# RWKV-7 attention with a squared-ReLU feed-forward layer: second layer's weights rounded later, feed-forward part begun one slot earlier, squares one step later

## The chip, the cores and the metric

The kernel runs on one core of one Trainium2 chip. The metric is the device time of one execution in microseconds (us). TensorE (PE) multiplies matrices, VectorE (DVE) and ScalarE (ACT) work elementwise, GpSimd (POOL) does a triangular solve here, and SyncE (SP) issues most of the transfers (DMA). Every engine works through its own instructions in the order in which the program lists them, and waits at the first one whose inputs are not there.

## The reference

```python
# attention: B, H, S, D = 4, 8, 768, 40
for t in range(S):
    y[:, :, t] = einsum('bhd,bhde->bhe', r_t, state)
    Sa = einsum('bhde,bhe->bhd', state, a_t)
    state = state * w_t - einsum('bhd,bhe->bhde', Sa, b_t) + einsum('bhd,bhe->bhde', v_t, k_t)
x = y.transpose(0, 2, 1, 3).reshape(3072, 320)
# feed-forward: w_in is 320 x 2048, w_out is 2048 x 320
h = maximum(x @ w_in, 0)
out = (h * h) @ w_out
```

`w_in` and `w_out` come as 64-bit floats, the other inputs as 32-bit floats. The kernel turns the 64-bit words into 32-bit floats itself, from their integer halves.

## The kernel before

The sequence is cut into 6 chunks of 128 steps for each of 4 batches: 24 pairs (chunk, batch), each handled in one *slot*. A barrier in the program's order separates slots; it costs no time by itself. What a slot holds is listed in the main loop:

```python
    TOTAL = 12
    ahead = {0: (4, 5), 1: (6, 7), 2: (8,), 3: (9,), 4: (10, 11), 5: (12, 13)}
    ahead.update({i: (i + 8,) for i in range(6, len(order) - 8)})
    share = {**{i: (0, 0) for i in range(B)}, B: (8, 4)}
    pieces_in = {0: (4, TOTAL), 1: (6, TOTAL), 2: (6, TOTAL), 3: (7, TOTAL), B: (4, 4)}
    for i in range(len(order)):
        n, begin = share.get(i, (10, 0))
        jobs = [(chain(i, g), 11, 0, TOTAL)]                     # the recurrence of this slot
        jobs.append((some(second, n), n, begin, TOTAL))          # n steps of the feed-forward part
        # prepare(m) for m in ahead[i]                           # decays and products of later slots
        # rest(i + 1)                                            # inputs of the next slot
        # rounding: 2 half-steps for each piece in pieces_in[i]  # weights from 64 to 32 bits
        weave(*jobs)                                             # spreads each job over 12 steps
        # when all of a unit's prepared slots are done: solve(unit) on GpSimd
```

The weights are rounded in 26 pieces: 10 wide ones of 512 columns for the first layer, then 16 of 320 columns, one for each 128 rows of `w_out`. A piece takes two ACT operations and five DVE operations. `hid` is the later home of the hidden layer, which lends room to the raw words until then; the numbers of finished pieces in `then` start the next fetch:

```python
    in_turn = [free_words[:, at:at + 2 * DM] for at in [4 * WI + 2 * DM * i for i in range(4)] + [2 * DM * i for i in range(3)]]
    ...
    def rounding():
        ...
            if before:
                nc.scalar.activation(bits, bits, Act.Relu, bias=lowest, scale=float(1 << 23))
            if n < len(pieces):
                nc.scalar.activation(dst, words[:, :, 0].bitcast(U32), Act.Copy, scale=2.0 ** -32)
            yield
            if before:
                nc.vector.scalar_tensor_tensor(d_.bitcast(I32), hi, -(1 << 31), bits, Alu.bitwise_and, Alu.bitwise_or)
                nc.vector.scalar_tensor_tensor(d_, mant, 2.0 ** -20, d_, Alu.mult, Alu.mult)
                # fetches of `then`
            if n < len(pieces):
                bits, mant = (psum(ps_f)[:, :dst.shape[-1]] for _ in range(2))
                nc.vector.tensor_scalar(bits, hi, 20, 0x7FF, Alu.logical_shift_right, Alu.bitwise_and)
                nc.vector.tensor_scalar(mant.bitcast(I32), hi, 0xFFFFF, 0x100000, Alu.bitwise_and, Alu.bitwise_or)
                nc.vector.tensor_tensor(mant, mant.bitcast(I32), dst, Alu.add)
            yield
```

The pool `ps_f` has two PSUM buffers, and the feed-forward part uses the same two. That part works on groups of three slots (384 tokens): 16 hidden steps, then three times 4 output steps of 4 matmuls each, 28 steps in all.

```python
    def ffn():
        for gi in range(len(order) // GB):
            while gi not in gathered or finished[0] < NARROW:
                yield False                                      # a step given away
            for f in range(0, NF, 2):
                ...                                              # two matmuls with w_third, for f and f + 1
                for e, p_ in enumerate(ps):
                    ...                                          # two matmuls with w_in
                    h_ = hidden[:, f + e]
                    nc.scalar.activation(h_, p_, Act.Relu)
                    nc.vector.tensor_tensor(h_, h_, h_, Alu.mult)
                    yield True
            while left():
                yield False                                      # until every piece is rounded
            for n in range(GB):
                ...                                              # 16 matmuls with w_out, a yield after every 4
                nc.scalar.copy(o_, p_); store(out[at:at + C, :], o_)
                yield True
```

At the end of every third slot the three slots' tokens are moved into the feed-forward part's layout by eight small transfers (`tokens<-tokens`); `gathered` is set two steps after these are listed. GpSimd's solve of a unit of 1, 2 or 4 slots reads its input back from HBM (`half_n<-kept_d`), works in `half_p` and `half_t`, and stores the result (`kept_t<-half_t`); the slots fetch it as `T<-kept_t`, over the queue of SyncE.

```python
    sizes = [1, 1] + [2] * 4 + [4] * ((len(order) - 12) // 4) + [2]   # units 0 to 9
    ...
            nc.gpsimd.tensor_tensor(p_, part[...], t3[...], Alu.mult)        # half_p
            nc.gpsimd.tensor_tensor(t3[...], t3[...], p_, Alu.subtract)      # half_t
```

Of the kernel before, what the change touches and what calls it, by code (L numbers as in the profile page):

```python
# [9 lines left out]
I32 = mybir.dt.int32  # L10
U32 = mybir.dt.uint32
Alu = mybir.AluOpType
# [5 lines left out]
def kernel(  # L18
# [22 lines left out]
    nc = tc.nc  # L41
    ctx.enter_context(tc.manual_schedule())
    B, H, S, D = r.shape
    DM = H * D
# [3 lines left out]
    HC = C // 2  # L48
# [3 lines left out]
    NF = DFF // 128  # L52
# [7 lines left out]
    at = 0  # L60
    for h, d, n in ((6, 0, D), (7, 0, D), (5, HALF, D - HALF)):
        while n:
            j, row, room_ = free[at]
            m_ = min(n, room_)
# [3 lines left out]
            d, n = d + m_, n - m_  # L68
# [11 lines left out]
    ps_f = ctx.enter_context(tc.tile_pool(name="ps_f", bufs=2, space=PSUM))  # L80

    def psum(pool):
        name = "ps_" + pool.name[-1]
        return pool.tile([128, 512], FP32, tag=name, name=name)

    def mm(o, l_, r_, start):
        nc.tensor.matmul(o, l_, r_, start=start, stop=True, skip_group_check=True)  # L87

    def single(name, shape):
        return const.tile(shape, FP32, tag=name, name=name)  # L90

    def new(name, shape, bufs):
        return work.tile(shape, FP32, tag=name, name=name, bufs=bufs)
# [4 lines left out]
    def later(fn, steps=2):  # L98
        line.append([steps, fn])
# [7 lines left out]
    def store(out_, in_, steps=2, queue=nc.sync):  # L107
        later(lambda: queue.dma_start(out=out_, in_=in_), steps)  # L108
# [77 lines left out]
    w_out = single("w_out", [128, NF, DM])  # L186

    WI = 512
# [9 lines left out]
    free_words = hidden.rearrange("p f t -> p (f t)")  # L198
# [1 line left out]
    nc.vector.memset(lowest, -896.0 * (1 << 23))  # L200
    wide = [room[:, 4 * WI * i:4 * WI * (i + 1)] for i in range(2)] + [free_words[:, :4 * WI]]

    in_turn = [free_words[:, at:at + 2 * DM] for at in [4 * WI + 2 * DM * i for i in range(4)] + [2 * DM * i for i in range(3)]]
    LENT = len(in_turn)


    runs = []
# [19 lines left out]
    NARROW = len(pieces)  # L227
    WIDE = len(fetches)
    for f in range(NF):
        fetchable(in_turn[f % LENT], [(0, 128, moe_w_out[f * 128:(f + 1) * 128, :])], [w_out[:, f, :]])  # L230

    then = {1: (3,), 2: (WIDE,), 3: (4,), 4: (WIDE + 1,), 5: (WIDE + 2,), 6: (WIDE + 3,), 7: (WIDE + 4,), 8: (WIDE + 5,),
            9: (WIDE + 6,)}
    then.update({NARROW + f: (WIDE + f + LENT,) for f in range(NF - LENT)})
    finished = [0]
    left = lambda: len(pieces) - finished[0]

    def fetch_weights(n, queue):
        raw, sources = fetches[n]
        for row, m_, src in sources:  # L240
            to = raw.bitcast(I32)[row:row + m_]
            if len(src.shape) == 3:
                to = to.rearrange("p (i c) -> p i c", i=src.shape[1])
            queue.dma_start(out=to, in_=src.bitcast(I32))

    def rounding():

        now = None
        for n in range(len(pieces) + 1):
            before, now = now, None  # L250
            if before:
                bits = before[-1]
                nc.scalar.activation(bits, bits, Act.Relu, bias=lowest, scale=float(1 << 23))
            if n < len(pieces):
                dst, raw = pieces[n]
                words = raw.rearrange("p (f e) -> p f e", e=2)
                nc.scalar.activation(dst, words[:, :, 0].bitcast(U32), Act.Copy, scale=2.0 ** -32)
            yield
            if before:
                d_, hi, mant, bits = before  # L260
                nc.vector.scalar_tensor_tensor(d_.bitcast(I32), hi, -(1 << 31), bits, Alu.bitwise_and, Alu.bitwise_or)  # L261
                nc.vector.scalar_tensor_tensor(d_, mant, 2.0 ** -20, d_, Alu.mult, Alu.mult)
                finished[0] += 1
                for m_ in then.get(n - 1, ()):
                    later(lambda m_=m_: fetch_weights(m_, nc.sync), 1)
            if n < len(pieces):
                hi = words[:, :, 1].bitcast(I32)
                bits, mant = (psum(ps_f)[:, :dst.shape[-1]] for _ in range(2))
                bits = bits.bitcast(I32)
                nc.vector.tensor_scalar(bits, hi, 20, 0x7FF, Alu.logical_shift_right, Alu.bitwise_and)  # L270
                nc.vector.tensor_scalar(mant.bitcast(I32), hi, 0xFFFFF, 0x100000, Alu.bitwise_and, Alu.bitwise_or)
                nc.vector.tensor_tensor(mant, mant.bitcast(I32), dst, Alu.add)
                now = dst, hi, mant, bits
            yield

    def as_they_are():
# [13 lines left out]
    Q = HC // 2  # L290
# [102 lines left out]


    given = single("half_n", [128, Q * (HC + Q)])
    solved = single("half_t", [128, Q * HC])

    part_of = lambda u: given[:, u % 3 * Q * Q:(u % 3 + 1) * Q * Q] if u < FINE else given

# [245 lines left out]

    PART = NF // 4

    def ffn():
        for gi in range(len(order) // GB):
            while gi not in gathered or finished[0] < NARROW:  # L650
                yield False
            t_ = tokens.pop(gi)
            hid = []
            for f in range(0, NF, 2):
                ps = [psum(ps_f if gi < len(order) // GB - 1 else ps_w)[:, :GB * C] for _ in range(2)]
                for e, p_ in enumerate(ps):
                    half = slice(e * DP, (e + 1) * DP)
                    mm(p_, w_third[half, f * 64:f * 64 + 128], t_[half, NT, :], True)
                for e, p_ in enumerate(ps):
                    for j in range(NT):  # L660
                        mm(p_, w_in[:, j, (f + e) * 128:(f + e + 1) * 128], t_[:, j, :], False)
                    h_ = hidden[:, f + e]
                    nc.scalar.activation(h_, p_, Act.Relu)  # L663
                    nc.vector.tensor_tensor(h_, h_, h_, Alu.mult)  # L664
                    hid.append(h_)
                    yield True
            while left():
                yield False
            for n in range(GB):
                bb, c = order[gi * GB + n]  # L670
                p_ = psum(ps_f if gi < len(order) // GB - 1 else ps_w)[:, :DM]
                for f in range(NF):
                    mm(p_, hid[f][:, n * C:(n + 1) * C], w_out[:, f], f == 0)
                    if f % PART == PART - 1 and f < NF - 1:
                        yield True
                o_ = new("o", [128, DM], 2)
                nc.scalar.copy(o_, p_)
                at = bb * S + c * C
                store(out[at:at + C, :], o_)
                yield True  # L680

    second = ffn()
    gathered = set()

# [92 lines left out]
    TOTAL = 12  # L779
    ahead = {0: (4, 5), 1: (6, 7), 2: (8,), 3: (9,), 4: (10, 11), 5: (12, 13)}  # L780
    ahead.update({i: (i + 8,) for i in range(6, len(order) - 8)})
    share = {**{i: (0, 0) for i in range(B)}, B: (8, 4)}
    pieces_in = {0: (4, TOTAL), 1: (6, TOTAL), 2: (6, TOTAL), 3: (7, TOTAL), B: (4, 4)}
    done = set(range(B))
    unit = unit_of[B]
    for i in range(len(order)):
        bb, c = order[i]
        n, begin = share.get(i, (10, 0))
# [13 lines left out]
        if i in pieces_in:  # L802
            m_, end = pieces_in[i]
# [39 lines left out]
```

## Time and profile before

| | before |
|---|---|
| median of 3 runs | 1058.01 us (1055.46 to 1059.7) |
| span of the profiled run | 1058.2 us |
| PE busy | 943.7 us, 89% |
| POOL busy | 668.4 us, 63% |
| DVE busy | 500.5 us, 47% |
| ACT busy | 272.4 us, 26% |
| mean granted TensorE clock | 0.901 |

A slot ends where DVE scales its output (`tokens<-ps_c,dec`, L636). In this profile slot 0 ends at 89.7 us, slots 1 to 5 end at 139.0, 184.7, 222.8, 268.5 and 319.0 us, and slot 23 ends at 989.7 us. After that the last group of the feed-forward part stands alone. PE is the engine with the most busy time, but matmuls are pipelined and their ends are modelled, so that a busy PE is not always PE at its peak. GpSimd's spans are rough.

### The profile page before, as it was taken

How to read it: one execution, taken by the hardware profiler on the slowest of the kernel's cores; microseconds unless marked ns; L12 is line 12 of the kernel's file. 1: busy time of each engine (PE TensorE's matmuls, PEld its weight loads, DVE VectorE, ACT ScalarE, POOL GpSimd, SP SyncE). 2: the span in 40 equal slices, each digit the busy share in tenths (PEclk: the TensorE clock that was granted, in tenths of full speed). 3: DMA queues.
4: the chain of work that ended last, by engine and by line, in shares of the span. 5: the costliest groups of instructions: out<-in, count | busy, mean ns of one | idle time of the engine just before them, and what ended most of it. 6: DMA issues, size and time to landing. Idle time of an engine off the chain costs nothing.

```text
span 1058.2 us, 19794 instructions
## 1 busy us (share of the span) xinstructions
PE 943.7 (89%) x7824; PEld 684.2 (65%) x7824; DVE 500.5 (47%) x940; ACT 272.4 (26%) x627; POOL 668.4 (63%) x1124
## 2 busy tenths in 40 slices
PE   6375767778999999999999999999998999999898
PEld 5264566665667766776677667766676677667556
DVE  5456786786463465543662563365323322331120
ACT  3133332442322223113212323113212311231120
POOL 4788564885898699981899952999958980000000
PEclk8656555578889999999999999999999999999899
DMA  8878978757547737248627429514344433310000
GB/s 110 163 141 173 182 210 166 178 139 169 113 82 142 176 40 147 73 67 213 136 40 152 109 56 198 129 22 114 62 108 102 70 77 88 73 24 7 22 1 19
DMA packets 261356, 113.51 MB, mean 107 GB/s; under 512 B 243792, under 2 KB 249424, under 8 KB 259600
## 3 DMA queue, kind: packets, MB, share of 16 engines
q1 hardware_dynamic: 256928, 93.24, 43.9%
q0 software_dynamic: 3248, 18.88, 7.3%
q8 instruction: 62, 1.02, 0.4%
q10 hardware_dynamic: 1088, 0.13, 0.1%
q14 instruction: 30, 0.25, 0.1%
HBM read 75.77 MB, written 34.48 MB: 104 GB/s over the span
## 4 chain that ended last, share of the span: by engine, by line
PE 74%; DMA 8%; DVE 7%; issue 3%; ACT 3%; POOL 3%; SPq 2%; DVEq 0%; ACTq 0%; POOLq 0%
PE ps_f L87 36%; PE ps_c L87 16%; PE ps_w L87 15%; PE ps_w L311 4%; SPq L108 2%; DMA dec<-kept_e 2%; DMA w_out<-in_moe_w_in_dram 1%; POOL half_t L434 1%; POOL half_p L432 1%; PE ps_c L577 1%; DMA in_b<-in_b_dram 1%; DVE decay L352 1%; DMA tokens<-tokens 1%; DMA in_w<-in_w_dram 1%; DVE decay L353 1%
## 5 line engine op out<-in xcount | busy, mean ns | idle before, releaser
L432 POOL TENSOR_TENSOR half_p<-half_n,half_t 128x70 f32<-128x70 f32 (+52 forms) x502 | 297.8, 593 | 103.7 <-DMA half_n<-kept_d 53.5
L434 POOL TENSOR_TENSOR half_t<-half_t,half_p 128x70 f32<-128x70 f32 (+52 forms) x502 | 323.3, 644 | 39.3
L664 DVE TENSOR_TENSOR hid<-hid 128x384 f32<-128x384 f32 x128 | 92.5, 723 | 242.1 <-ACT hid L663 242.0
L87 PE MATMUL ps_f<-w_out,hid 128*128 128x320 f32 x672 | 200.4, 441 | 0.0
L87 PE MATMUL ps_f<-tokens,w_in 128*128 128x384 f32 x448 | 176.4, 517 | 0.0
L87 PEld LDWEIGHTS ps_f<-w_out,hid 128*128 128x128 f32 x672 | 120.9, 190 | 45.6 <-issue 2.9
L663 ACT ACTIVATE hid<-ps_f 128x384 f32<-128x384 f32 x112 | 54.9, 490 | 260.4 <-PE ps_f L87 260.4
L87 PEld LDWEIGHTS ps_f<-tokens,w_in 128*128 128x128 f32 x448 | 77.4, 193 | 65.4 <-issue 34.6
L87 PE MATMUL ps_f<-tokens,w_third 64*128 64x384 f32 x224 | 56.0, 539 | 3.2 <-DVE w_out L261 3.2
L87 PE MATMUL ps_w<-decay,bT 40*128 40x128 f32 x352 | 31.5, 329 | 27.4 <-DVE decay L357 27.4
L327 DVE TENSOR_TENSOR A<-ps_w,upper 128x512 f32<-128x512 f32 x48 | 30.9, 685 | 43.0 <-PE ps_w L87 43.0
L87 PEld LDWEIGHTS ps_w<-decay,bT 40*128 40x128 f32 x352 | 26.7, 226 | 36.4 <-DVE decay L357 20.6
L348 DVE TENSOR_TENSOR_SCAN decay<-ps_w,ones 128x64 f32<-128x64 f32 x88 | 23.5, 267 | 51.0 <-PE ps_w L311 51.0
L87 PE MATMUL ps_w<-dec,kvT 40*128 40x128 f32 x384 | 31.9, 309 | 17.1 <-DVE kvT L503 17.1
L327 DVE TENSOR_TENSOR RX<-ps_w,upper 128x512 f32<-128x512 f32 x48 | 30.8, 682 | 33.5 <-PE ps_w L87 33.3
L503 DVE TENSOR_TENSOR kvT<-ps_w,dec 128x512 f32<-128x512 f32 x24 | 16.4, 684 | 58.4 <-PE ps_w L311 37.5
L87 PEld LDWEIGHTS ps_w<-dec,kvT 40*128 40x128 f32 x384 | 27.0, 210 | 22.2 <-DVE kvT L503 19.8
L87 PEld LDWEIGHTS ps_c<-xr,T 64*64 64x64 f32 x768 | 29.5, 148 | 15.6 <-issue 10.0
L87 PEld LDWEIGHTS ps_w<-rT,kvT 40*128 40x128 f32 x384 | 27.9, 204 | 17.3 <-DVE RX L327 8.8
L87 PE MATMUL ps_w<-rT,kvT 40*128 40x128 f32 x384 | 33.5, 305 | 6.0 <-DVE RX L327 4.6
L327 DVE TENSOR_TENSOR RV<-ps_w,upper 128x512 f32<-128x512 f32 x48 | 30.9, 685 | 15.8 <-PE ps_w L87 15.4
L87 PE MATMUL ps_w<-rT,xnT 40*128 40x128 f32 x384 | 35.1, 293 | 3.6 <-ACT rT L513 2.9
(139 smaller groups left out, 1433.9 us busy)
## 6 DMA issues: line engine op xcount, KB each, us to landing
kept_e<-decay SPq DMA_DIRECT2D x22, 780.0 KB
dec<-kept_e SPq DMA_DIRECT2D x22, 780.0 KB
hid<-in_moe_w_out_dram SPq DMA_DIRECT2D x16, 320.0 KB
half_n<-kept_d POOLq DMA_DIRECT2D x12, 384.0 KB, 9.9
half_n<-kept_d POOLq DMA_DIRECT2D x6, 768.0 KB, 10.8
in_w<-in_w_dram SPq DMA_DIRECT2D x24, 160.0 KB
in_ab<-in_b_dram SPq DMA_DIRECT2D x24, 160.0 KB
in_ab<-in_a_dram SPq DMA_DIRECT2D x24, 160.0 KB
```

The costliest lines, as they stand in the source:

```text
L87: nc.tensor.matmul(o, l_, r_, start=start, stop=True, skip_group_check=True)
L108: later(lambda: queue.dma_start(out=out_, in_=in_), steps)
L311: nc.tensor.transpose(p_[:, q * 128:(q + 1) * 128], pair(x_, q), ident)
L327: nc.vector.tensor_tensor(t_, p_, over4(upper), Alu.mult)
L348: nc.vector.tensor_tensor_scan(up[:, q, MID + 1:C + 1], wT[:, q, MID:], ones, 1.0, Alu.mult, Alu.mult)
L352: nc.vector.reciprocal(down[:, :, MID + 1:C + 1], up[:, :, MID + 1:C + 1])
L353: nc.vector.reciprocal(up[:, :, :MID], down[:, :, :MID])
L432: nc.gpsimd.tensor_tensor(p_, part[:, at:at + m_].unsqueeze(1).to_broadcast([128, n, m_]), t3[:, :n, s:s + 1].to_broadcast([128, n, m_]), ...
L434: nc.gpsimd.tensor_tensor(t3[:, :n, s + 1:], t3[:, :n, s + 1:], p_, Alu.subtract)
L503: nc.vector.tensor_tensor(kT, kT_, down[:, :, 1:C + 1], Alu.mult)
L663: nc.scalar.activation(h_, p_, Act.Relu)
L664: nc.vector.tensor_tensor(h_, h_, h_, Alu.mult)
```

## The change

The change has four parts.

- **Rounding later.** Slots 0 to 3 round 3, 4, 4 and 6 pieces in place of 4, 6, 6 and 7; slot 4 rounds 6 in place of 4, and slot 5 rounds the last ones. Fetches of raw words move with them.
- **Other places for raw and half-done words.** Raw words go to rows of `w_out` that are not rounded yet, to free tiles of the solve (`half_t`) and to the output tiles, so that `hid` is free earlier. The exponent `bits` is written to the result's own place in SBUF, and `mant` of the pieces from number 11 on goes to `half_t` in SBUF, not to a buffer of `ps_f`.
- **The feed-forward part begins in slot 3** (4 steps from step 6 on), and slot 4 begins its 8 steps at step 2, not 4.
- **The square of a hidden step is listed one step later**, after the next step's matmuls and ReLU.

```diff
+    solved = single("half_t", [128, 2048])
+    outputs = single("o", [128, 2, DM])
+    aside, temporary = solved[:, 1024:1024 + 2 * DM], solved[:, 1024 + 2 * DM:1024 + 3 * DM]
+    rows_of = lambda f: w_out[:, f:f + 2].rearrange("p f c -> p (f c)")
+    in_turn = [free_words[:, at:at + 2 * DM] for at in [4 * WI + 2 * DM * i for i in range(4)]]
+    in_turn += in_turn[:2] + [rows_of(f) for f in (8, 10, 12, 14)]
+    in_turn += [aside, outputs.rearrange("p n c -> p (n c)"), rows_of(14), aside]
+    in_turn += [outputs.rearrange("p n c -> p (n c)"), aside]
...
-    then = {1: (3,), 2: (WIDE,), 3: (4,), 4: (WIDE + 1,), 5: (WIDE + 2,), 6: (WIDE + 3,), 7: (WIDE + 4,), 8: (WIDE + 5,),
-            9: (WIDE + 6,)}
-    then.update({NARROW + f: (WIDE + f + LENT,) for f in range(NF - LENT)})
+    then = {1: (3,), 3: (4,)}
+    for n, fs in {4: (0,), 5: (1,), 6: (2,), 7: (3,), 9: (6, 7), 10: (4, 8), 11: (5, 9), 14: (10,), 15: (11,), 19: (12,),
+                  20: (13,), 21: (14,), 23: (15,)}.items():
+        then[n] = tuple(WIDE + f for f in fs)
+
+    LATE = NARROW + 1
...
-                d_, hi, mant, bits = before
-                nc.vector.scalar_tensor_tensor(d_.bitcast(I32), hi, -(1 << 31), bits, Alu.bitwise_and, Alu.bitwise_or)
+                d_, hi, mant = before
+                nc.vector.scalar_tensor_tensor(d_.bitcast(I32), hi, -(1 << 31), d_.bitcast(I32), Alu.bitwise_and, Alu.bitwise_or)
                 nc.vector.scalar_tensor_tensor(d_, mant, 2.0 ** -20, d_, Alu.mult, Alu.mult)
...
-                bits, mant = (psum(ps_f)[:, :dst.shape[-1]] for _ in range(2))
-                bits = bits.bitcast(I32)
-                nc.vector.tensor_scalar(bits, hi, 20, 0x7FF, Alu.logical_shift_right, Alu.bitwise_and)
+                mant = psum(ps_f)[:, :dst.shape[-1]] if n < LATE else temporary
                 nc.vector.tensor_scalar(mant.bitcast(I32), hi, 0xFFFFF, 0x100000, Alu.bitwise_and, Alu.bitwise_or)
                 nc.vector.tensor_tensor(mant, mant.bitcast(I32), dst, Alu.add)
+                nc.vector.tensor_scalar(dst.bitcast(I32), hi, 20, 0x7FF, Alu.logical_shift_right, Alu.bitwise_and)
...
                     nc.scalar.activation(h_, p_, Act.Relu)
-                    nc.vector.tensor_tensor(h_, h_, h_, Alu.mult)
+                    if hid:
+                        square(hid[-1])
                     hid.append(h_)
                     yield True
+            square(hid[-1])
...
-    share = {**{i: (0, 0) for i in range(B)}, B: (8, 4)}
-    pieces_in = {0: (4, TOTAL), 1: (6, TOTAL), 2: (6, TOTAL), 3: (7, TOTAL), B: (4, 4)}
+    share = {**{i: (0, 0) for i in range(B - 1)}, B - 1: (4, 6), B: (8, 2)}
+    pieces_in = {0: (3, TOTAL), 1: (4, TOTAL), 2: (4, TOTAL), 3: (6, TOTAL), 4: (6, TOTAL), 5: (4, 5)}
```

More of the change, by code (lines that the diff above doesn't have):

```diff
@@ L201 @@
     wide = [room[:, 4 * WI * i:4 * WI * (i + 1)] for i in range(2)] + [free_words[:, :4 * WI]]
-    in_turn = [free_words[:, at:at + 2 * DM] for at in [4 * WI + 2 * DM * i for i in range(4)] + [2 * DM * i for i in range(3)]]
-    LENT = len(in_turn)
+    solved = single("half_t", [128, 2048])
[6 more added lines that the diff above has]
+    in_turn += [outputs.rearrange("p n c -> p (n c)"), aside]
     runs = []
@@ L229 @@
     for f in range(NF):
-        fetchable(in_turn[f % LENT], [(0, 128, moe_w_out[f * 128:(f + 1) * 128, :])], [w_out[:, f, :]])
-    then = {1: (3,), 2: (WIDE,), 3: (4,), 4: (WIDE + 1,), 5: (WIDE + 2,), 6: (WIDE + 3,), 7: (WIDE + 4,), 8: (WIDE + 5,),
-            9: (WIDE + 6,)}
-    then.update({NARROW + f: (WIDE + f + LENT,) for f in range(NF - LENT)})
-    finished = [0]
+        fetchable(in_turn[f], [(0, 128, moe_w_out[f * 128:(f + 1) * 128, :])], [w_out[:, f, :]])
+    then = {1: (3,), 3: (4,)}
[3 more added lines that the diff above has]
+    LATE = NARROW + 1
+    finished, fetched = [0], set()
     left = lambda: len(pieces) - finished[0]
@@ L239, in fetch_weights @@
         raw, sources = fetches[n]
+        fetched.add(n)
         for row, m_, src in sources:
@@ L251, in rounding @@
             if before:
-                bits = before[-1]
+                bits = before[0].bitcast(I32)
                 nc.scalar.activation(bits, bits, Act.Relu, bias=lowest, scale=float(1 << 23))
@@ L255, in rounding @@
                 dst, raw = pieces[n]
+                assert (n // 2 if n < NARROW else WIDE + n - NARROW) in fetched
                 words = raw.rearrange("p (f e) -> p f e", e=2)
@@ L264, in rounding @@
                 for m_ in then.get(n - 1, ()):
-                    later(lambda m_=m_: fetch_weights(m_, nc.sync), 1)
+                    if n < len(pieces) - 1:
+                        later(lambda m_=m_: fetch_weights(m_, nc.sync), 1)
+                    else:
+                        fetch_weights(m_, nc.sync)
             if n < len(pieces):
                 hi = words[:, :, 1].bitcast(I32)
-                bits, mant = (psum(ps_f)[:, :dst.shape[-1]] for _ in range(2))
-                bits = bits.bitcast(I32)
-                nc.vector.tensor_scalar(bits, hi, 20, 0x7FF, Alu.logical_shift_right, Alu.bitwise_and)
+                mant = psum(ps_f)[:, :dst.shape[-1]] if n < LATE else temporary
                 nc.vector.tensor_scalar(mant.bitcast(I32), hi, 0xFFFFF, 0x100000, Alu.bitwise_and, Alu.bitwise_or)
                 nc.vector.tensor_tensor(mant, mant.bitcast(I32), dst, Alu.add)
-                now = dst, hi, mant, bits
+                nc.vector.tensor_scalar(dst.bitcast(I32), hi, 20, 0x7FF, Alu.logical_shift_right, Alu.bitwise_and)
+                now = dst, hi, mant
             yield
@@ L395 @@
     given = single("half_n", [128, Q * (HC + Q)])
-    solved = single("half_t", [128, Q * HC])
     part_of = lambda u: given[:, u % 3 * Q * Q:(u % 3 + 1) * Q * Q] if u < FINE else given
@@ L646 @@
     PART = NF // 4
+    square = lambda h_: nc.vector.tensor_tensor(h_, h_, h_, Alu.mult)
     def ffn():
@@ L675, in ffn @@
                         yield True
-                o_ = new("o", [128, DM], 2)
+                o_ = outputs[:, n % 2]
                 nc.scalar.copy(o_, p_)
```

## The prediction

> **What bounds the kernel now.** I read the page's slices first, then the busy time slot by slot, then who waited for whom, then stretches of the timeline.
>
> ```profile
> PE   6375767778999999999999999999998999999898
> DVE  5456786786463465543662563365323322331120
> PEclk8656555578889999999999999999999999999899
> ```
>
> Each digit is a slice of 26.5 us. From slice 10 on PE is full at full clock; before that it is 60 to 80% busy at 0.5 to 0.8 of the clock.
>
> By slot (columns: PE, weight loads, DVE, ACT, POOL busy with counts; clock; DMA share; GB/s), slots 1, 2, 3, 4, 5, 9 and 10, then the tail:
>
> ```profile
> 89.70:139.00 49.30, 33.94 (x312) 29.35 (x313) 34.92 (x65) 16.18 (x35) 32.60 (x88) 0.50 0.94 187
> 139.00:184.70 45.70, 31.23 (x302) 27.04 (x300) 31.85 (x60) 14.06 (x33) 21.96 (x58) 0.59 0.84 190
> 184.70:222.80 38.10, 28.62 (x296) 24.62 (x296) 30.39 (x67) 14.85 (x36) 34.01 (x53) 0.64 0.63 149
> 222.80:268.50 45.70, 39.19 (x367) 29.48 (x368) 31.59 (x72) 16.65 (x40) 32.39 (x74) 0.78 0.69 157
> 268.50:319.00 50.50, 46.64 (x410) 33.01 (x409) 27.03 (x52) 14.59 (x34) 45.17 (x69) 0.86 0.52 102
> ...
> 437.20:477.50 40.30, 40.06 (x338) 30.30 (x337) 14.51 (x31) 7.50 (x18) 34.65 (x47) 1.00 0.47 105
> 477.50:516.00 38.50, 36.92 (x322) 25.14 (x321) 19.38 (x39) 11.33 (x26) 14.39 (x26) 1.00 0.74 160
> ...
> 989.70:1058.20 68.50, 62.49 (x206) 36.06 (x205) 8.93 (x16) 9.54 (x20) 0.00 (x0) 0.94 0.04 14
> ```
>
> In slots 1 and 2 the DMA engines are nearly full and DVE is at 70%; in slot 3 DVE is at 80%. Slot 4 is between; from slot 5 on PE is the bound, and little is left idle. Most of what is left, of PE alone in 319 to 990 us (us, times, longest):
>
> ```profile
> PE ps_w L87 <- DVE kvT L503: 14.2, 10, 2.0
> PE ps_w L87 <- ACT rT L513: 2.4, 10, 0.2
> ```
>
> **GpSimd is the second bound.** Unit 6 (slots 10 to 13) is asked for as soon as unit 5 has ended, and its result meets slot 10 closely:
>
> ```profile
> 341.75 1.03 POOL L409 DMA_DIRECT2D half_n<-kept_d  x2 [0.17 <-DMA in_w<-in_w_dram]
> ...
> 475.07 0.60 POOL L437 DMA_DIRECT2D kept_t<-half_t  x1 [0.30 <-POOL half_t L434]
> 480.57 2.34 SPq L448 DMA_DIRECT2D T<-kept_t  x2
> ```
>
> The first matmul with this T starts at 491.36 us. GpSimd went from 170.96 (unit 4) to 475.07 without waiting for a slot; only after that does it wait 14 and 17 us for `kept_d`.
>
> **What the Trainium skill says.** "SBUF — State Buffer", section "Who interferes with whom": a DVE instruction with two SBUF inputs shares a read path with GpSimd, one of the two has to wait for the whole other instruction, and a tensor_scalar from SBUF to SBUF may do so too. The trace agrees. These are the 126 operations of two solves of one shape, unit 4 with 1 square beside it, unit 9 with 16:
>
> ```profile
> L434 POOL TENSOR_TENSOR half_t<-half_t,half_p 128x252 f32<-128x252 f32 (+52 forms) x63 | 34.8, 553 | 4.9
> L432 POOL TENSOR_TENSOR half_p<-half_n,half_t 128x252 f32<-128x252 f32 (+52 forms) x63 | 32.5, 516 | 17.4 <-DMA half_n<-kept_d 12.5
> ```
> ```profile
> L434 POOL TENSOR_TENSOR half_t<-half_t,half_p 128x252 f32<-128x252 f32 (+52 forms) x63 | 37.4, 593 | 4.9
> L432 POOL TENSOR_TENSOR half_p<-half_n,half_t 128x252 f32<-128x252 f32 (+52 forms) x63 | 33.7, 536 | 11.7 <-DMA half_n<-kept_d 6.9
> ```
>
> That is 67.3 against 71.1 us, 0.25 us for each square. "TensorE: Matmul & The Clock Gate", section "What's actually happening": PE runs at half clock until it has been busy for some microseconds. The clock of 0.50 to 0.64 in slots 1 to 3 fits; steps put into slot 3 are dear at first and warm the clock.
>
> **Part by part.** *Unit costs.* The page has 112 hidden steps in `ps_f` for 176.4 + 56.0 us, 2.08 us each, and 84 output steps for 200.4 us, 2.39 us each. A narrow piece is five DVE operations of 0.48 to 0.50 us, 2.4 us; a wide one five of 0.66 to 0.70 us, 3.4 us. A fetch of raw `w_out` rows is 0.33 MB, at the 187 GB/s of slot 1 about 1.75 us of all engines.
>
> *Rounding moved.* Slot 0 loses one wide piece, with DVE at 83% there (19.8 of 23.7 us): -2.5. Slot 1 loses two wide pieces (6.8 us of DVE) and, by the fetch tables, three fetches (5 us of DMA); its chain runs through transfers of `in_k` and `in_b` (13.5 us) and through stores that wait for DVE, so I take most of the larger one and some of the other: -8. Slot 2 swaps six narrow pieces for three wide and one narrow (-2 us of DVE) and loses two fetches (3.5 us): -4. Slot 4 has three more pieces, 7 us of DVE on 31.6, less the release of `ps_f`: +2.5, with its earlier steps. Slot 5 has 27 us of DVE in 50.5, so that its three pieces fit beside PE; it has 9 steps of the feed-forward part before its last product in place of 10, and late squares: -4.
>
> *Begin in slot 3.* Four steps are offered, two stand before the slot's last product. At a clock of 0.64 two hidden steps cost 6.5 us of PE, and 9.5 us are idle, but the slot's DVE, at 80%, has the squares and slower SBUF operations on top: +4. Slots 0 to 5 come to -2.5 - 8 - 4 + 4 + 2.5 - 4 = -12.
>
> *Squares later.* Where a hidden step stands ahead of `kvT`, DVE waits at the square for ReLU, and PE then waits for `kvT`: 1.4 us, ten times. The late square frees DVE. Slots 7 and 8 give 3.3 us back; the remaining 11 I take at three quarters, 8.
>
> *Where the moved steps go.* In the built program's order of matmuls, slots 6 to 9 hold 41 steps in place of 39 (+4.3), slots 10 to 23 hold 136 in place of 139 (-6.4), and the tail 28 in place of 30. So PE alone would reach slot 10's T at -12 + 4.3 - 3.3 = -11, at 480.4 us.
>
> *The solve.* Unit 4 may begin 10.5 us earlier (slots 0 and 1). But 15 narrow pieces have each five operations from SBUF to SBUF, three with two SBUF inputs. At the square's rate (0.25 us of loss for 0.56 us) one costs GpSimd 0.2 us: 0.6 to 1 us a piece, 12 for all, and 1.5 for earlier squares. Unit 6 ends at 475 - 10.5 + 13.5 = 478. A store of this kind lands 4.4 us after its issue (list of transfers), the two loads take 1.3 us to issue and, in slot 18, 2.5 us to land: some 8 us, so T at 486. PE waits 5.6 us, and only 5.4 us of the gain pass slot 10.
>
> *New waits for tokens.* Groups 5 and 6 now begin right behind the slot whose tokens they need: one output step and a few transposes, then hidden steps, in slots 18 and 21. Before, four or five output steps stood between. The eight transfers take 6 us and more to issue, and the tail shows what a group that begins at once has to wait:
>
> ```profile
> 989.72 6.25 SPq L108 DMA_DIRECT2D tokens<-tokens  x8
> ...
> 996.15 2.99 PE L87 MATMUL ps_w<-tokens,w_third 64*128 64x384 f32 x4 [2.69 <-DMA tokens<-tokens]
> ```
>
> That is 8 us from slot end to tokens at the least; 3.5 to 4 us of work stand ahead: +4.5 in slot 21, +4 in slot 18, where 1.5 us of waiting for T end in it.
>
> *Tail.* The two output steps fewer stood where PE waits for the last tokens (989 to 993.5, then idle to 996): 0.
>
> *Sum.* -5.4 up to slot 10, then -6.4 - 8 + 8.5 = -5.9: -11.3 in all, 1046.7. I say 1046 us.
>
> **Rivals.** (1) The solve isn't in the way and contention is mild: then 11 us pass slot 10, and a better slot 1 (it holds 15 us without PE) makes 20 to 25: 1033. For it: GpSimd's start moves with slot 1. Against: it had 8 us of slack at slot 10 (475 + 8 = 483, used at 491), no more. (2) Contention is heavy: if each of the 75 SBUF operations costs GpSimd its own half microsecond, 37 us less the overlap, T comes 10 to 15 us later than I have it, SyncE's queue stands still behind it, and the early gain is gone: 1060. For it: single solve operations stretch from 0.5 to 0.9 us beside a square. Against: the mean is 0.25. (3) The moved steps simply fill idle PE (8.6 us) and nothing else happens: 1049. Against: the tail is bounded by tokens, not by the two steps.
>
> **Range and chances.** The early slots are uncertain by 8 us, the solve by 10, the token waits by 5: about 13 together. Range 1031 to 1061. Faster by 2% means under 1036.8: 0.27. Slower by 2% needs more than every bad rival together: 0.04.
>
> **What would show it.** Right: slot 1 some 8 us shorter at a lower DMA share; slot 5 ending near 307; hardly any wait of PE for `kvT`; unit 4's and unit 5's operations longer than 67 and 70 us; SyncE waiting for `kept_t` in slot 10; PE waiting for `tokens` in slots 18 and 21. Wrong: slots 1 and 2 as long as before (then their bound is neither weights nor DVE); slot 10 without a wait (then more is gained); the tail shorter than 68.5 us.

## The result and the profile after

The changed kernel takes 1073.1 us (median of 4 runs, 1068.86 to 1075.72) where the kernel before took 1056.8 us beside it (1055.46 to 1059.7). The ratio is 1.0147, with a 95% interval of 1.0099 to 1.0194: slower by 1.5%. Predicted were 1046 us, and 1061 at the most. The profiled run is the fastest of the four, with a span of 1067.2 us against 1058.2, so that the profile shows 9 us of a loss that is 15 us in the ratio.

The slices of the profile after:

```profile
PE   6375677889989999998999999999959998999798
DVE  5445578799752574362553653366114322331120
PEclk7566566589879999998999999999979998999899
```

Counted from 0, slices of 26.7 us: PE is a little fuller in most of slices 5 to 9 than before, as the feed-forward part begins earlier, but slices 10 and 11 (slot 5) have a clock of 0.8 and 0.7, and slice 29 (slot 18) is half empty. DVE's fullest slices are now 8 and 9.

Slots 1, 2, 4, 5, 10 and 18 of the changed kernel, then the tail (columns: stretch, length, PE, weight loads, DVE, ACT, POOL busy with counts, clock, DMA share, GB/s):

```profile
86.88:141.76 54.88, 35.32 (x330) 30.56 (x328) 31.48 (x60) 14.20 (x32) 37.45 (x95) 0.56 0.96 175
141.76:181.15 39.39, 27.38 (x292) 23.52 (x292) 28.94 (x51) 13.27 (x30) 20.36 (x54) 0.68 0.81 170
...
218.94:259.80 40.86, 37.90 (x384) 27.79 (x381) 38.87 (x79) 18.88 (x45) 33.80 (x63) 0.92 0.85 180
259.80:318.79 58.99, 50.11 (x412) 36.80 (x411) 41.58 (x78) 17.20 (x40) 46.60 (x77) 0.80 0.54 118
...
473.20:518.08 44.88, 40.69 (x318) 26.77 (x317) 20.05 (x41) 11.41 (x26) 20.63 (x40) 0.89 0.66 146
779.85:827.45 47.60, 36.43 (x287) 23.07 (x285) 13.27 (x26) 9.18 (x21) 33.73 (x65) 0.86 0.51 112
...
997.98:1067.20 69.22, 59.45 (x192) 33.92 (x192) 8.94 (x16) 9.13 (x19) 0.00 (x0) 0.92 0.04 11
```

Slots 0 to 4 together end 8.7 us earlier than before (259.8 against 268.5). Slot 5 takes it back: 59.0 us in place of 50.5, with DVE busy for 41.6 us in place of 27.0. Slot 10 lasts 6.5 us longer, slot 18 9.3 us. These three lose 24 us, the other slots together gain some 16. Slot 18 before:

```profile
782.29:820.58 38.29, 35.45 (x301) 24.76 (x301) 11.48 (x22) 8.16 (x19) 26.58 (x53) 1.00 0.54 119
```

The tail is as long as it was.

The chain of work that ended last, by engine:

```profile
PE 53%; POOL 28%; DMA 8%; issue 4%; SPq 2%; DVE 2%; ACT 1%; POOLq 0%; ACTq 0%; DVEq 0%
```

Before, PE had 74% of it and GpSimd 3%. So the path to the end now runs through GpSimd's solve for more than a quarter of the time.

What PE waited for from 319 us to the end (us, times, longest; the second row is in the tail):

```profile
PE ps_f L87 <- DMA tokens<-tokens: 14.3, 3, 10.7
PE ps_w L87 <- DMA tokens<-tokens: 7.2, 1, 7.2
PE ps_c L87 <- DMA T<-kept_t: 4.0, 1, 4.0
```

The 14.2 us of waiting for `kvT` are gone; waits for tokens and for T stand in their place. The 14.3 us are 11.2 in slot 18 (10.7 and 0.4) and 3.2 in slot 21. In the tail PE waited 2.7 us before. **Slot 10**, from the timeline (start, duration, engine, line):

```profile
481.86 0.60 POOL L450 DMA_DIRECT2D kept_t<-half_t  x1 [0.30 <-POOL half_t L447]
...
490.26 1.08 PE L87 MATMUL ps_c<-xr,T 64*64 64x40 f32 x16 [3.95 <-DMA T<-kept_t]
```

GpSimd stores unit 6 at 481.9 us, 6.8 us later than before, while PE wants T 5 us earlier (at 486.3 us in place of 491.4). SyncE's queue meanwhile stands still for 11.0 us at the fetch of this T. **Slot 5**, its waits for the products of the decays (us, times, longest), then the stretch around the largest:

```profile
PE ps_w L87 <- DVE decay L371: 7.5, 2, 5.4
...
293.20 1.69 DVE L367 RECIPROCAL decay<-decay 128x256 f32<-128x256 f32 x1
294.81 0.56 DVE L273 SCALAR_TENSOR_TENSOR w_out<-half_t,w_out 128x320 int32<-128x320 int32 x1
295.40 0.77 DVE L274 SCALAR_TENSOR_TENSOR w_out<-half_t,w_out 128x320 f32<-128x320 f32 x1
296.10 1.04 DVE L661 TENSOR_TENSOR hid<-hid 128x384 f32<-128x384 f32 x1
297.06 0.68 DVE L370 TENSOR_TENSOR bT<-ps_w,decay 128x512 f32<-128x512 f32 x1
297.66 0.68 DVE L371 TENSOR_TENSOR decay<-ps_w,decay 128x512 f32<-128x512 f32 x1
298.39 2.08 PE L87 MATMUL ps_w<-decay,bT 40*128 40x128 f32 x16 [5.43 <-DVE decay L371]
```

DVE is not idle in these rows. Between the reciprocals and the two products (`bT`, `decay`) that PE waits for stand two operations of rounding and a square, 2.4 us, and just ahead of the reciprocals another piece and a square, 4.7 us from 286.8 to 291.5. PE waits 5.4 us (1.9 at the most before), and the slot's clock is 0.80, where before it was 0.86.

**Slot 18**, where the tokens of group 5 (slots 15 to 17) are wanted at once:

```profile
778.64 0.60 POOL L450 DMA_DIRECT2D kept_t<-half_t  x1 [0.30 <-POOL half_t L447]
779.34 1.95 POOL L422 DMA_DIRECT2D half_n<-kept_d  x4
779.88 13.63 SPq L108 DMA_DIRECT2D tokens<-tokens  x8
793.07 1.62 PE L87 MATMUL ps_f<-tokens,w_third 64*128 64x384 f32 x2 [10.73 <-DMA tokens<-tokens]
```

The eight transfers took 13.6 us to issue, where other groups take 6.3. They stand beside GpSimd's store of a solved unit (1 MB) and its loads of the next one (four of 0.38 MB). The same row in the trace before and in that of run 2 (below):

```profile
782.32 11.25 SPq L108 DMA_DIRECT2D tokens<-tokens  x8
...
810.55 6.36 SPq L108 DMA_DIRECT2D tokens<-tokens  x8
```

Before, PE did not wait for these tokens, as output steps stood between. In run 2 the transfers come 13 us after GpSimd's store, and PE waits 4.6 us.

### The profile page after: what moved, and what is told of

Same layout as the page of the kernel before. It is cut to its first block, busy times and chain, and to the rows that moved or that the text cites. A ratio compares the mean times of both kernels' runs of the same rounds, so it can differ in the third digit from the quotient of the medians.

```text
span 1067.2 us, 19776 instructions
## 1 busy us (share of the span) xinstructions
PE 951.2 (89%) x7824; PEld 684.8 (64%) x7824; DVE 509.5 (48%) x940; ACT 272.8 (26%) x627; POOL 680.9 (64%) x1124
## 4 chain that ended last, share of the span: by engine, by line
PE 53%; POOL 28%; DMA 8%; issue 4%; SPq 2%; DVE 2%; ACT 1%; POOLq 0%; ACTq 0%; DVEq 0%
PE ps_f L87 26%; POOL half_t L447 14%; POOL half_p L445 13%; PE ps_w L87 12%; PE ps_c L87 10%; DMA half_n<-kept_d 3%; PE ps_w L325 3%; SPq L108 2%; DMA tokens<-tokens 1%; DMA in_k<-in_k_dram 1%; PE ps_c L619 1%; DMA w_out<-in_moe_w_in_dram 1%; DMA kept_n<-N 1%; POOL half_n L422 1%; PE ps_c L590 1%
## 5 line engine op out<-in xcount | busy, mean ns | idle before, releaser
L445 POOL TENSOR_TENSOR half_p<-half_n,half_t 128x70 f32<-128x70 f32 (+52 forms) x502 | 304.5, 607 | 104.0 <-DMA half_n<-kept_d 52.2
L447 POOL TENSOR_TENSOR half_t<-half_t,half_p 128x70 f32<-128x70 f32 (+52 forms) x502 | 328.3, 654 | 39.4
L87 PE MATMUL ps_f<-w_out,hid 128*128 128x320 f32 x672 | 202.8, 445 | 0.0
L87 PE MATMUL ps_f<-tokens,w_in 128*128 128x384 f32 x448 | 179.3, 524 | 0.0
L87 PE MATMUL ps_f<-tokens,w_third 64*128 64x384 f32 x224 | 61.1, 561 | 14.3 <-DMA tokens<-tokens 14.3
L87 PEld LDWEIGHTS ps_c<-xr,T 64*64 64x64 f32 x768 | 30.1, 150 | 19.3 <-issue 13.3
L87 PE MATMUL ps_c<-xr,T 64*64 64x40 f32 x768 | 36.1, 243 | 6.2 <-DMA T<-kept_t 4.0
L366 DVE RECIPROCAL decay<-decay 128x256 f32<-128x256 f32 x22 | 38.3, 1741 | 0.0
L367 DVE RECIPROCAL decay<-decay 128x256 f32<-128x256 f32 x22 | 37.3, 1693 | 0.0
L87 PEld LDWEIGHTS ps_f<-tokens,w_third 64*128 64x128 f32 x224 | 23.0, 196 | 22.0 <-issue 20.0
```

Of the source, the lines that this page charges most:

```text
L366: nc.vector.reciprocal(down[:, :, MID + 1:C + 1], up[:, :, MID + 1:C + 1])
L367: nc.vector.reciprocal(up[:, :, :MID], down[:, :, :MID])
L445: nc.gpsimd.tensor_tensor(p_, part[:, at:at + m_].unsqueeze(1).to_broadcast([128, n, m_]), t3[:, :n, s:s + 1].to_broadcast([128, n, m_]), ...
L447: nc.gpsimd.tensor_tensor(t3[:, :n, s + 1:], t3[:, :n, s + 1:], p_, Alu.subtract)
```

## The experiments

Eleven kernels ran. Each ratio is to the kernel before, run beside it on the same chip, where its median was 1060.7 to 1062.1 us.

**1. Only the late squares, in the kernel before.**

```diff
                     nc.scalar.activation(h_, p_, Act.Relu)
-                    nc.vector.tensor_tensor(h_, h_, h_, Alu.mult)
+                    if hid:
+                        nc.vector.tensor_tensor(hid[-1], hid[-1], hid[-1], Alu.mult)
                     hid.append(h_)
                     yield True
+            nc.vector.tensor_tensor(hid[-1], hid[-1], hid[-1], Alu.mult)
```

> The kernel before with the late squares alone. Theory (late squares help, the loss comes from elsewhere): PE's 14.2 us of waiting for kvT in 319 to 990 us go to nearly zero and the time falls by 8 to 12 us, to 1045 to 1049. Rival (late squares are themselves a loss, because each square now stands in DVE's line behind the next ReLU, or because the freed time is lost again at the tokens and at T): 1055 or more.

Measured: 1046.13 us, ratio 0.9843 (0.98 to 0.9885). PE no longer waits for `kvT`. Slots 5 and 10 of this run:

```profile
264.47:307.62 43.15, 41.90 (x410) 29.91 (x409) 27.22 (x53) 14.56 (x34) 38.48 (x60) 0.96 0.63 119
462.07:507.72 45.65, 41.48 (x321) 27.36 (x321) 18.84 (x39) 11.35 (x26) 21.93 (x43) 0.89 0.64 147
```

Slot 5 takes 43.2 us in place of 50.5 with the same 27 us of DVE: here the order of the operations on DVE counts, not their number. Slot 10, reached 15.4 us earlier, waits 3.9 us for T, and slot 18 5.5 us. This part alone brings more than I had given to all four.

**2. The changed kernel with its squares listed where they were.**

```diff
-                    if hid:
-                        square(hid[-1])
+                    square(h_)
                     hid.append(h_)
                     yield True
-            square(hid[-1])
```

> The changed kernel with the squares put back beside their ReLU. The late squares alone gave the kernel before 1.6% (15 us). Theory (they are worth as much here, since DVE is even fuller): 12 to 20 us slower than the changed kernel, PE waits for kvT back, about 1088. Rival (most of their gain is swallowed by the waits for tokens and for T that stand behind): under 6 us slower.

Measured: 1098.77 us, ratio 1.0332 (1.0267 to 1.0396), slot 5 at 65.3 us. The wait is back, longer than before:

```profile
PE ps_w L87 <- DVE kvT L516: 19.6, 11, 4.0
```

From 1.0332 to 1.0147 the squares bring 1.8% in the changed kernel too. So the other three parts cost about 3% together, and the loss has to be found in them.

**3. The changed kernel without the arithmetic of the last four pieces.** The products use twelve of the sixteen row blocks of `w_out`, four of them twice, so that the work on PE stays; ACT and DVE of four pieces are left out.

```diff
-            if n < len(pieces):
+            if n < len(pieces) - 4:
                 dst, raw = pieces[n]
...
-                    mm(p_, hid[f][:, n * C:(n + 1) * C], w_out[:, f], f == 0)
+                    mm(p_, hid[f][:, n * C:(n + 1) * C], w_out[:, f % (NF - 4)], f == 0)
```

> The changed kernel without the arithmetic on the last four pieces (raw words are still fetched, the last four blocks of 128 rows of the second layer's weights are replaced by the first four, so the output lacks them). Theory (the rounding in slot 5 stands in DVE's line ahead of the decay products that PE waits for): slot 5 shrinks from 59.0 us to 46 to 50, the PE waits of 2.0 and 5.4 us for L371 there go, and the time falls by 6 to 10 us against the changed kernel, to about 1064. Part of it may be taken back by T in slot 10. Rival (slot 5 is long for another reason, the PE clock of 0.80 or the output steps): slot 5 stays above 55 us and the time within 4 us of the changed kernel.

Measured: 1068.32 us, ratio 1.007 (1.0049 to 1.0091). Slots 5 and 10:

```profile
259.91:306.37 46.46, 42.90 (x411) 31.84 (x410) 28.18 (x58) 13.64 (x32) 35.67 (x63) 0.93 0.71 149
460.79:514.43 53.64, 38.35 (x318) 25.45 (x317) 20.54 (x40) 11.52 (x26) 29.00 (x51) 0.87 0.54 122
```

Slot 5 falls from 59.0 to 46.5 us at a clock of 0.93: the last pieces cost it 12.5 us. But slot 10 grows by 8.8 us and now waits 13.5 us for T. GpSimd gives back only 2.4 us (unit 6 stored at 479.4 in place of 481.9), so that most of what slot 5 gains is lost at slot 10. The gain on the changed kernel is 4.8 us by the medians, where 6 to 10 were expected, and 0.8% by the ratios.

**4. Less lead into the later token waits.** Slots 16 and 17 get 8 steps of the feed-forward part in place of 10; the steps are listed later.

```diff
-    share = {**{i: (0, 0) for i in range(B - 1)}, B - 1: (4, 6), B: (8, 2)}
+    share = {**{i: (0, 0) for i in range(B - 1)}, B - 1: (4, 6), B: (8, 2), 16: (8, 0), 17: (8, 0)}
```

> The changed kernel with 8 steps in place of 10 in slots 16 and 17, so that groups 5 and 6 begin behind four and more output steps as they did before. Theory (the lead of the feed-forward part runs into the gathering of the tokens): the 14.3 us of PE waiting for tokens go to under 4, slot 18 returns from 47.6 to 38 to 40 us and slot 21 to 34 to 35, and the time falls by 8 to 12 us, to about 1063. Rival (the wait only changes its place, since the same tokens are late for slot 18's T as well): under 4 us of gain.

Measured: 1055.37 us, ratio 0.9941 (0.9916 to 0.9966): 17.7 us less than the changed kernel, where 8 to 12 were expected. PE waits for tokens for 3.1 us from 319 us to the end, tail included, where the changed kernel waits 14.3 and 7.2:

```profile
PE ps_w L87 <- DMA tokens<-tokens: 3.1, 2, 2.7
```

The difference is 18.4 us of waiting. Slot 18 waits 5.8 us for T in their place, and its clock is 0.92 where the changed kernel has 0.86, so that these waits alone are not the whole account. The slot:

```profile
784.46:825.40 40.94, 35.11 (x291) 24.12 (x290) 11.25 (x23) 7.75 (x18) 27.69 (x56) 0.92 0.59 130
```

Slot 18 takes 40.9 us in place of 47.6, slot 21 33.1 in place of 37.0; slots 16 to 22 together are 19.3 us shorter. Slot 14 is 7.3 us longer, though up to slot 15 the two programs are the same: in this execution a transfer (`dec<-kept_e`) landed late there, and PE waited 4.1 us for `kvT`, which needs it. So one slot can differ by 7 us from one execution to another, and the profile as a whole won 10.8 us.

**5. The old begin of the feed-forward part, all else as changed.**

```diff
-    share = {**{i: (0, 0) for i in range(B - 1)}, B - 1: (4, 6), B: (8, 2)}
+    share = {**{i: (0, 0) for i in range(B)}, B: (8, 4)}
```

> The changed kernel with the feed-forward part begun as before (slot 4 at step 4, nothing in slot 3). Theory (the earlier begin only builds up a lead that nothing can use): token waits go as with less lead, slots 3 and 4 get shorter or stay, and since the last two steps only fill the tail's wait for tokens the time falls by 8 to 14 us, to about 1061. Rival (the earlier begin is worth its 8.6 us of moved PE work, and the loss is the rounding's): the same time as the changed kernel or more.

Measured: 1055.57 us, ratio 0.9942 (0.9917 to 0.9968), with no wait for tokens in the middle stretch and slot 5 still at 59.1 us. It is the same time as in the run before: with the earlier begin undone, or with its lead taken off ahead of slot 18, the kernel is 2% faster. The earlier begin itself, with its steps in slots 3 and 4, is worth nothing that can be seen between these two runs; its lead costs 2%. And the 59 us of slot 5 don't come from the earlier begin.

**6. Only the new places and the late squares.** Old begin, old pace of rounding.

```diff
-    share = {**{i: (0, 0) for i in range(B - 1)}, B - 1: (4, 6), B: (8, 2)}
-    pieces_in = {0: (3, TOTAL), 1: (4, TOTAL), 2: (4, TOTAL), 3: (6, TOTAL), 4: (6, TOTAL), 5: (4, 5)}
+    share = {**{i: (0, 0) for i in range(B)}, B: (8, 4)}
+    pieces_in = {0: (4, TOTAL), 1: (6, TOTAL), 2: (6, TOTAL), 3: (7, TOTAL), B: (4, 4)}
```

> The changed kernel with the begin and the pace of the rounding of before (4, 6, 6, 7 and 4 pieces in slots 0 to 4): of the change only the other places of words and the late squares are left. Theory (what made the kernel with the old begin 9 us slower than late squares alone is the pace, which leaves four pieces to slot 5): the time comes back to 1044 to 1050, slot 5 to 43 to 45 us. Rival (it is the places: rounding from SBUF to SBUF stands in GpSimd's way and makes DVE slower): 1052 or more, unit 4's solve still 6 us longer and slot 10 waiting for T by 5 us more than with late squares alone.

Measured: 1050.85 us, ratio 0.99 (0.984 to 0.9959), just above the expected 1044 to 1050, with slot 5 at 44.3 us and slot 1 at 45.7. Between this and the run before lies only the pace: 0.4%, with intervals that overlap. In the traces the later rounding brings 6.3 us up to the end of slot 4 (265.8 us in run 5, 272.1 here), and slot 5 then takes 14.8 us more (59.1 and 44.3). Between this and the first run lie only the places: 0.6%, not resolved either. What the trace shows of the places is unit 4: 83.1 us from its first operation to its store, as in the changed kernel (83.7); without the new places it takes 77.4 us, before and in the first run alike. Slot 10 does not wait for T here all the same.

**7. The late squares, with unit 6 split in two.** A unit of two slots should come earlier than one of four, and free slot 10.

```diff
-    sizes = [1, 1] + [2] * 4 + [4] * ((len(order) - 12) // 4) + [2]
+    sizes = [1, 1] + [2] * 6 + [4] * 2 + [2]
```

> The kernel before with late squares, and with the unit of slots 10 to 13 solved as two units of two slots (sizes 1, 1, six times 2, twice 4, 2), which costs GpSimd some 40 us more in all but has slot 10's T some 40 us earlier. Theory (GpSimd's solve bounds slot 10 once the slots before are shorter): slot 10 falls from 45.7 to 38 to 39 us, and the time by 5 to 8 us against late squares alone, to about 1040. Rival (GpSimd has no 40 us to spare, and T comes late in a later slot): slots 14 or 18 grow by what slot 10 wins, 1046 or more.

Measured: 1084.15 us, ratio 1.021 (1.016 to 1.026). Slot 10 is free (36.9 us), but slot 14 takes 86.8:

```profile
PE ps_c L87 <- DMA T<-kept_t: 46.1, 2, 41.7
```

The wait has moved from slot 10 (3.9 us in the first run) to slot 14 (41.7). My theory was wrong, and the rival right: from first operation to last store, two units of two slots take GpSimd 177 us, where one of four took 121 in the first run, and it has no such time to spare.

**8. The split together with run 3.** The edits of runs 3 and 7.

> The changed kernel without the arithmetic on the last four pieces (output as described for that run before) and with the split unit. Theory (slot 5's rounding costs 12.5 us, of which slot 10's wait for T hid 8.7): slot 10 falls from 53.6 to 39 to 40 us, and the time to about 1055, 8 to 14 us under the run without the split. Rival: the wait moves on to slot 12 or 14, under 4 us.

Measured: 1100.02 us, ratio 1.0368 (1.0313 to 1.0423); slot 10 36.1 us, slot 14 88.4. About 1055 was expected. The same as in run 7, on top of another kernel.

**9. Run 3 and run 4 together**: no last rounding, less lead.

> The changed kernel with less lead (8 steps in slots 16 and 17) and without the arithmetic on the last four pieces (output as described for the earlier run without it). Theory (the two losses are separate: the tokens' wait about 18 us by the medians, slot 5's rounding about 8 us net of slot 10): both together take 22 to 28 us off the changed kernel, to 1046 to 1051, that is the time of late squares alone. Rival (they are the same loss seen twice, since every delay before slot 18 is absorbed there): no better than less lead alone, 1055.

Measured: 1052.99 us, ratio 0.9936 (0.9912 to 0.9959), no better than less lead alone (0.9941). Slot 5 has its 45.9 us, but slot 10 needs 54.7, and PE waits for T for 13.7 us there and 6.1 in slot 18. This missed the expectation of 1046 to 1051: what slot 5 gains doesn't arrive, as GpSimd is not ready.

**10. The first run, with T and N of slots 14, 18 and 22 fetched over ScalarE's queue**, so that SyncE's doesn't stand still.

```diff
-        joining = inverses(i, g) if i else iter(())
+        joining = inverses(i, g, nc.scalar if i in (14, 18, 22) else nc.sync) if i else iter(())
```

> Late squares alone, and the T and N of slots 14, 18 and 22 loaded over ScalarE's queue, not behind the tokens in SyncE's. Theory (slot 18's wait of 5 us for T is the queue's, since its solve had ended before): slot 18 falls from 43.6 to 37 to 39 us, and the time by 4 to 6 us, to about 1041. Rival (the load itself or ScalarE's wait for it is what takes the time): 1045 or more, with ScalarE standing still at the load.

Measured: 1042.72 us, ratio 0.9851 (0.982 to 0.9881). It has the lowest median of all, but the ratio can't be told from the first run's. In the trace slots 17 and 18 take 75.2 us in place of 79.4, and slot 10 47.2 in place of 45.7. Inconclusive.

**11. The changed kernel mended**: pieces spread over slots 0 to 4 as 4, 5, 5, 6, 7 with none in slot 5, less lead as in run 4, and the queue as in run 10.

```diff
-    pieces_in = {0: (3, TOTAL), 1: (4, TOTAL), 2: (4, TOTAL), 3: (6, TOTAL), 4: (6, TOTAL), 5: (4, 5)}
+    pieces_in = {0: (4, TOTAL), 1: (5, TOTAL), 2: (5, TOTAL), 3: (6, TOTAL), 4: (7, TOTAL)}
```

> The changed kernel with its losses mended: rounding over in slot 4 (4, 5, 5, 6 and 7 pieces), less lead, and the queue as in the run beside it. Theory (what remains of the change beside late squares is the other places and the earlier begin, worth little, and 6 us more of solve): 1042 to 1050, slot 5 at 43 to 47 us, no wait for tokens in slots 18 and 21. Rival (the begin in slot 3 is worth its steps once its harm is gone): below the run beside it by 4 us or more.

Measured: 1054.82 us, ratio 0.9953 (0.9935 to 0.9971), where 1042 to 1050 were expected. Slot 5 is mended (44.4 us), but slot 4, now with seven pieces, takes 50.0, and slots 10 and 18 take 49.3 and 48.6 and wait 11.5 us for T. So even with less lead and no piece in slot 5, the changed kernel does not reach the late squares alone.

## Why the prediction was wrong

Two steps failed: the pieces in slot 5, whose mechanism was wrong, and the waits for tokens, whose size was. In the profile slot 5 and slots 11 to 23 are off by 12 us each; by the runs the tokens weigh more. I had a sum of -11.3 us, and the profile came to +9.0. The difference of 20.3 us, stretch by stretch, in us:

| | predicted | profile after | off by |
|---|---|---|---|
| slots 0 to 4 | -8 | -8.7 | -0.7 |
| slot 5 | -4 | +8.5 | +12.5 |
| slots 6 to 9 | +1 | -4.1 | -5.1 |
| slot 10, wait for T | +5.6 | +6.5 (4.0 of it waiting) | +0.9 |
| slots 11 to 23 | -5.9 | +6.2 | +12.1 |
| tail | 0 | +0.7 | +0.7 |

- **"Slot 5 has 27 us of DVE in 50.5, so that its three pieces fit beside PE … -4" is the step whose mechanism failed.** I compared a busy time with the length of a slot. DVE works in the program's order, and slot 5 holds two chains (reciprocals, `bT`, `decay`) for which PE waits; a piece that is listed in between delays them, however idle DVE is elsewhere. The last four pieces cost slot 5 12.5 us (run 3), in PE's waiting and at a lower clock, and the first run shows the other side: the same 27 us of DVE, in a better order, make the slot 7.4 us shorter. Runs 5 and 6, with only the pace between them, say the same of rounding later as a whole: "Rounding moved" was to bring 16 us up to the end of slot 5, and in the traces it brings 6.3 up to slot 4 and loses 14.8 in slot 5. In the ratio this error is mostly hidden, as slot 10 takes back what slot 5 gains: leaving the pieces out brings 0.8% (run 3), and with less lead nothing that can be seen (0.9936 in run 9 against 0.9941).
- **"New waits for tokens … +4.5 in slot 21, +4 in slot 18" had the mechanism right and the size wrong, and this weighs most in the result.** In place of 8.5 us PE waits 14.3: 3.2 in slot 21 and 11.2 in slot 18. I took 6.25 us of issue from the tail for both. In slot 18 the eight transfers meet GpSimd's change of units and take 13.6 us; away from it, in run 2, they take 6.4. The 11.25 us of the same row before would have told. The tail's wait grew as well, from 2.7 to 7.2 us, about the time of the two output steps that had stood there. By runs 4 and 5 the whole lead costs 2% (18 us by the medians, 22 by the ratios), and the waits for tokens that go in run 4 come to 18.4 us, against 5.8 us of waiting for T that come. The lower clock behind a wait (0.86 in slot 18) may make up the difference; that is not shown apart. With less lead the changed kernel takes 1055.4 us, without its last pieces 1068.3.
- **"Slots 0 to 5" is right in its sum up to slot 4 and wrong in its parts.** Slot 1 was to be 8 us shorter; it is 5.6 us longer, and slots 2 and 4 make up for it (6.4 and 4.9 us shorter, where -4 and +2.5 were predicted). There is less rounding in slot 1, but a raw fetch of 1 MB for the first layer (`w_out<-in_moe_w_in_dram`) is now issued at 103.6 us and not at 96.5 (in runs 6 and 11 at 96.6 and 96.8), just ahead of `in_k`, and the chain of waits of the profile after runs through that:

```profile
105.34 0.32 SPq L255
105.75 9.27 DMA in_k<-in_k_dram
```

  `in_k` lands 9.3 us after its issue; before, it took 3.7. I had counted the bytes that leave slot 1 (three fetches), but the DMA share there rose from 0.94 to 0.96. It is the slower pace that does this, not the list of fetches: slot 1 takes 54 to 55 us in every run with the new pace, and 45.7 and 46.8 in runs 6 and 11, which have the same list and round one piece more in slot 0 and one or two more in slot 1. That the one fetch ahead of `in_k` is the whole reason was not tried by itself.
- **"Squares later … 8" was too small.** The mechanism is right (no wait for `kvT` is left), but I took the gain from the 14.2 us of these waits. It is 1.6% alone (run 1) and 1.8% in the changed kernel (run 2), with 7 us of it in slot 5, where no such wait stood in my table, as that began at 319 us; PE's waits for `decay` in slot 5, 2.6 us before, are gone in the first run. Slots 6 to 9 are 4.1 us shorter in the first run too; by the count of matmuls they hold one step more in the changed kernel, where I had counted two (+4.3).
- **"The solve" came out near its end and not in its parts.** The 12 us of contention that I put on it by the Trainium skill, "SBUF — State Buffer", section "Who interferes with whom", are 6 in unit 4 (operations of 73.6 us in place of 67.3, from the group rows below) and none in unit 5, which takes 80.4 us from first operation to store, as before (80.5). DVE pays as well: a square about slot 5 takes 796 ns on average (660 before, 700 in the first run), and single ones 1.04 us. That agrees with the page in kind; its size is for each kernel to measure. The other half of the delay is in the start of unit 4, 1.6 us earlier in place of 10.5, as slot 1 didn't shrink. These two misses cancelled for the most part: unit 6 was stored at 481.9 us, 478 was predicted, and slot 10 lost what I had given it. Unit 4 after:

```profile
L447 POOL TENSOR_TENSOR half_t<-half_t,half_p 128x252 f32<-128x252 f32 (+52 forms) x63 | 37.7, 598 | 4.9
L445 POOL TENSOR_TENSOR half_p<-half_n,half_t 128x252 f32<-128x252 f32 (+52 forms) x63 | 35.9, 570 | 15.1 <-DMA half_n<-kept_d 10.2
```

- **"Tail: 0"** holds: 69.2 us against 68.5, with two steps fewer and a longer wait for tokens in their place.
- **Rival 2** (1060, SyncE's queue standing still behind T) came nearest and named a true wait, SyncE's 11.0 us at T, but not its size: it had T come 10 to 15 us later than the 486 us that I predicted, and PE used it at 490.3.

Three steps fewer and no wait for `kvT` should have brought slots 10 to 23 some 14 us, and slots 11 to 23 without 18 and 21 brought 5.6. By a count of the matmuls in the traces the steps fewer are nearly all in slots 18 and 21 (17 in place of 20); in the other slots only the waits for `kvT` were to be had, 7.5 us before. What stays open is whether the new places cost anything in time beyond the 6 us on GpSimd in unit 4. Keeping all half-done words in PSUM beside the earlier begin was not tried.

**The cause in short.** The late squares win 1.6 to 1.8%. The earlier begin runs the feed-forward part into its own token transfers and loses 2%. The rounding left for slot 5 loses 12.5 us there, of which the wait for GpSimd at slot 10 hides most (0.8% is left, or nothing that can be seen once the lead is gone). What the places lose is not resolved (0.6% between run 6 and the first). The best versions are the late squares alone, 0.9843, and the same with the own queue, 0.9851; both beat both kernels.

## What to carry to other kernels

An engine with idle time in a stretch has room for more work only where its program order leaves it: look at which later operation on that engine another one waits for, and list the new work behind it. Work that is done earlier gains nothing if the next input isn't there: ask for each handover (tokens, T) how far the consumer may run ahead, and read its latency at that place and not at another. And where two engines are near the bound, a gain on one before their meeting point is lost in a wait for the other, so measure each part of a change alone.

## What the runs showed of the hardware

- The same eight small transfers took 6.3 us to issue in most groups and 13.6 us beside GpSimd's 1 MB store and 1.5 MB of loads, and 6.4 us in run 2, where they came 13 us after that store; a single `in_k` transfer landed in 3.7 us, and in 9.3 us right behind a fetch of 1 MB.
- In slot 5 PE's mean clock went down with its waits: 0.80 with 7.5 us of waiting for `decay` (the longest 5.4), 0.93 with 2.3 us of it and without the last pieces, and 0.96 with none in the first run. That agrees with the Trainium skill, "TensorE: Matmul & The Clock Gate", section "What's actually happening", by which PE falls back to half clock after some microseconds without work. In slot 10 the order is less clear: 0.89 with 4.0 us of waiting for T, 0.87 with 13.5 in run 3 and 0.81 with 13.7 in run 9. By the page, a wait of PE can cost more than its own length; no run here measures it apart.
- DVE was busy for 38.9 of 40.9 us in slot 4 of the changed kernel, and that slot was 4.9 us shorter than before; in slot 5 it was busy for 41.6 of 59.0, and that slot was longer. A busy share alone told nothing of the loss.
